# Twelve instead of ten token tiles of a second matrix product by 2x2 blocks, with the first block sum made by an accumulating DMA

## Chip, core and metric

The kernel runs on one core of one Trainium2 chip. The metric is the device time of one execution in microseconds (us), lower is better. Three runs of the kernel before took 453.23, 453.87 and 454.25 us; their median is 453.87 us. Work is done by TensorE (PE, with its weight loads as PEld), VectorE (DVE), ScalarE (ACT) and GpSimd (POOL); SyncE (SP) issues most DMAs.

## What is computed

One transformer-like block on x of 2048 tokens by 448 channels, all in float32. A linear-attention part comes first; then a token-mixing MLP, whose two products are what matters here:

```python
h = _layernorm(x, axis=-1) * (1 + cb) + sb
h = _layernorm(h, axis=-1)                        # inside _B_ref
u = jnp.einsum("bsd,sf->bdf", h, w1) + b1         # first product over tokens, F = 1792
u = _gelu(u)
y = jnp.einsum("bdf,fs->bds", u, w2) + b2         # second product: 1792 -> 2048 tokens
x = x + gb * y.transpose(0, 2, 1)
```

The second product, y^T = w2^T u, is the stage that is changed: 16 tiles of 128 tokens by 448 channels, each a sum over 14 blocks of 128 hidden rows.

## The kernel before

**Precision.** A float32 operand is cut into a high part, rounded to the fast matmul type float32r, and a low part, the rest. `split` (lines 75 to 77) does it: ACT rounds (L76), DVE subtracts (L77).

**Plain tiles.** `load1`, `split1` and `mult1` (lines 967 to 983) take one block of 128 hidden rows for `n` neighbouring token tiles: one DMA from w2 (tile `q`, L969), one split into `qw`, and for each token tile three matmuls of 448 columns (`acc3`, lines 740 to 742: high x high, high x low, low x high). A tile pair (`n` = 2) therefore has 14 such steps of six matmuls, a single tile 14 steps of three. `out1` adds the finished tile to x (L1005) and stores it.

**Tiles by 2x2 blocks.** Two token tiles, and the hidden blocks in pairs (seven pairs), are taken together by a scheme with seven block products in place of eight and with sums of blocks ahead of them. The group index is `q` (tiles 2q and 2q+1), the product index `m` from 0 to 6. `load_quads` (L883 to L890) loads four block columns a11, a12, a21, a22 of w2, each as two DMAs of 4 and 3 blocks (256 and 192 KB, L889). The left operands of the products are, in order, a11, a12, s2, s1, s3, s4, a22, with s1 = a21 + a22, s2 = s1 - a11, s3 = a11 - a21, s4 = a12 - s2. `split7` (L906) cuts operand m into `a11h`/`a11l` and so on and then makes the sum that the table `PRODS` (L901) names beside it, on DVE (`sub`, L896). `mult7` (L916) runs one product: seven pairs of a matmul of 448 columns (high part, L928) and one of 224 columns (low part, L929), 14 matmuls. `out7` (L945) takes results away: ACT copies the accumulator at m = 0, 2, 3 (L934), DVE adds at m = 1, 4, 5 (`out2`, L938 to L940) and at m = 6 (L962, L963); tile 2q is stored after m = 5 and tile 2q+1 after m = 6 (L943, on SP's queue).

**Order.** All instructions are issued in the order in which the Python code runs (a manual schedule), one queue for each engine. Of the 16 token tiles, 0 to 9 go by blocks (`NS7 = 5` groups) and 10 to 15 by plain steps, as pairs (10, 11), (12, 13) and singles 14 and 15. The list `order` (lines 1009 to 1017) starts with 8 plain steps, goes on with the 35 products, among which 38 plain steps are spread evenly, and ends with 10 plain steps of tile 15:

```python
for n, (kind, p) in enumerate(order):
...
        load2(n + LOAD2)
        split2(n + SPLIT2)
        if n < len(order) - LAST:
            (mult7 if kind == "s" else mult1)(*p)
            (out7 if kind == "s" else out1)(*p)
```

So at entry n the loads are issued 12 entries ahead (`LOAD2`), the splits, with their sums, 4 ahead (`SPLIT2`), then the matmuls of entry n, then its results. A store waits on SP's queue for DVE, and the loads behind it in the queue wait with it. `fetch_x` (L1043) brings a parked x tile back. Tiles live in 76 equal slots of SBUF; a load also waits until the last reader of its slot is done.

**Ahead of the stage.** The first product over tokens (L740 to L742 with `up`) runs until about 319 us of the profile; `finish_u` (lines 842 to 875) turns its results into the right operands of the second product, and its last jobs run on ACT and DVE until about 329 us. POOL issues accumulating DMAs earlier in the kernel (L244, L376, L399, L405), each adding one SBUF tile into another; in this stage it issues none.

Of the kernel before, what the change touches and what calls it, by code (L numbers as in the profile page):

```python
# [11 lines left out]
ALU = mybir.AluOpType  # L12
# [5 lines left out]
NF = F // P  # L18
# [26 lines left out]
def block_kernel(ctx: ExitStack, tc: tile.TileContext, x, wqkv, wo, w1, b1, w2, b2, c, wmod, out):  # L45
    nc = tc.nc
# [15 lines left out]
    def slot(name, w=D, dt=F32, parts=P):  # L62
        return slots.tile([parts, w], dt, name=name, tag="slot", padded_shape=[P, 512])

    def tslot(name, dt=F32, parts=P, w=D):
        return tok.tile([parts, w], dt, name=name, tag="tok", padded_shape=[P, 512])
# [469 lines left out]
    for t in range(3, NT):  # L536
# [38 lines left out]
        if t == 4:  # L575
            for g in range(4):
                w = tslot(f"wo{g}", parts=G)
# [184 lines left out]
    for i in range(NT + LAG):  # L762
# [13 lines left out]
        t = i - LAG  # L776
# [54 lines left out]
    uparts = ctx.enter_context(tc.tile_pool(name="uparts", bufs=1, reuse_waits="tile"))  # L831
    HD = D // 2
    PAIRS, RS = NF // 2, ((0, 4), (4, 3))
    NS7 = 5
    uw, uops, ufull = {}, {}, {}

    def u_parts(r, name, src):
# [42 lines left out]
    raw2, hilo, acc2, cop = {}, {}, {}, {}  # L880
    QUADS = {"a11": (0, 0), "a12": (1, 0), "a21": (0, 1), "a22": (1, 1)}

    def load_quads(q):  # L883
        for name, (fo, to) in QUADS.items():
            raw2[q, name] = []
            for r0, n in RS:
# [2 lines left out]
                nc.sync.dma_start(w.rearrange("p (r c) -> p r c", c=P), w2v[fo, :, r0:r0 + n, c0:c0 + P])  # L889
                raw2[q, name].append(w)  # L890

    def sub(q, out, a, b, op=ALU.subtract, into=None):
        res = []
        for i, (r0, n) in enumerate(RS):
            w = raw2[q, into][i] if into else slot(f"{out}_{q}_{r0}", n * P)
            nc.vector.tensor_tensor(w, raw2[q, a][i], raw2[q, b][i], op=op)  # L896
            res.append(w)
        raw2[q, out] = res


    PRODS = (("a11", "b11", 0, ("s1", "a21", "a22", ALU.add)), ("a12", "b21", 1, ("s2", "s1", "a11")),  # L901
             ("s2", "t2", 0, ("s3", "a11", "a21", ALU.subtract, "a21")),
             ("s1", "t1", 2, ("s4", "a12", "s2", ALU.subtract, "a12")), ("s3", "t3", 0, None),
             ("s4", "b22", 2, None), ("a22", "t4", 0, None))

    def split7(q, m):  # L906
        a, _, _, add = PRODS[m]
        hilo[q, m] = []
        for w, (r0, nr) in zip(raw2[q, a], RS):
            h, l = slot(f"{a}h_{q}_{r0}", nr * P, F32R), slot(f"{a}l_{q}_{r0}", nr * P, F32R)  # L910
            split(w, h, l)
            hilo[q, m].append((h, l))
        if add:
            sub(q, *add)

    def mult7(q, m):  # L916
        a, b, k, _ = PRODS[m]
        opens = m in (0, 1, 3)
        if opens:
            acc2[q, k] = bank(f"y{q}_{k}")  # L920
        ps = acc2[q, k]
        closes = m in (1, 5, 6)
        cut = hilo.pop((q, m))
        for r in range(PAIRS):
            (h, l), i = cut[r // 4], r % 4
            w, wh = uops[b, r]
            s = slice(i * P, (i + 1) * P)
            nc.tensor.matmul(ps[:, :D], h[:, s], w, start=opens and r == 0, stop=False, skip_group_check=True)  # L928
            nc.tensor.matmul(ps[:, :HD], l[:, s], wh, start=False, stop=closes and r == PAIRS - 1,  # L929
                             skip_group_check=True)  # L930
# [76 lines left out]


    sevens = [(q, m) for q in range(NS7) for m in range(7)]
    plains = [(t, n, f) for t, n in ((10, 2), (12, 2), (14, 1), (15, 1)) for f in range(NF)]  # L1010
    LEAD, TAIL = 8, 10
    order = [("p", p) for p in plains[:LEAD]]
    mid = plains[LEAD:len(plains) - TAIL]
# [32 lines left out]
    for o0, n in W1G[1:]:  # L1046
# [5 lines left out]
        for r in range(first, NT):  # L1052
# [4 lines left out]
            if xleft and k % 2:  # L1057
                t = xleft.pop(0)
# [13 lines left out]
    for n, (kind, p) in enumerate(order):  # L1072
        if jobs:
            jobs.pop(0)()
        while xleft:
            t = xleft.pop(0)
# [42 lines left out]
```

## Time and profile before

| What | Value |
|---|---|
| Runs | 453.23, 453.87, 454.25 us; median 453.87 |
| The profiled execution | 452.57 us, of which the span of the core is 450.8 us; 1.77 us lie around it |
| PE busy in the span | 446.0 us (99%), granted clock 1.0 |
| Second product, first plain step to last product by blocks | 319.46 to 440.04 us |
| The 10 last plain steps, with the split-up last tile | 440.04 to 447.95 us |

Times in the profile count from the start of the span. A line of a group or timeline names the engine, the line of the code, the operation, and the output and input tiles by their names (`a11h` is the high part of a11, `y` an accumulator of a block product, `yp` one of a plain step). A matmul's duration in the timeline is its time in the pipeline; what it costs a stream of matmuls is the distance from its start to the next one's start.

### The profile page before, as it was taken

The page shows a single profiled execution, that of the slowest core. Times are in us where ns is not written, and L with a number is a line of the kernel's source. Part 1 is how long each engine was busy: PE and PEld are TensorE (multiplying, and loading weights), DVE is VectorE, ACT ScalarE, POOL GpSimd, SP SyncE. Part 2 cuts the span into 40 slices and gives each one's busy share as a digit, 9 for nine tenths or more (in the row PEclk, how much of TensorE's full clock was granted, in tenths as well). Part 3 has the DMA queues.
Part 4 walks back from the last instruction along what each step waited for, and adds up shares of the span by engine and source line. Part 5 has one row for each costly group of instructions (what it writes and reads, how often), then busy time and mean ns, then how long its engine had stood idle before and what let it go on. Part 6 is the DMA issues. An engine that isn't in the chain of part 4 may idle for free.

```text
span 450.8 us, 7295 instructions
## 1 busy us (share of the span) xinstructions
PE 446.0 (99%) x2385; PEld 411.0 (91%) x2385; DVE 356.0 (79%) x774; ACT 250.1 (55%) x559; POOL 89.0 (20%) x162
## 2 busy tenths in 40 slices
PE   9999999999999999999999999999999999999997
PEld 8689999989899999999999999999999999999997
DVE  5797787888899899896469677539696978798993
ACT  2659877755656576767675345236546262536350
POOL 2124675620014345554300000000000000000000
PEclk9999999999999999999999999999999999999999
DMA  8949899985200003222407463417960674628313
GB/s 216 308 113 205 148 188 248 223 203 163 72 0 2 23 25 104 62 49 48 138 28 242 135 203 100 132 36 233 279 184 24 197 224 125 168 100 254 111 58 100
DMA packets 60551, 61.64 MB, mean 137 GB/s; under 512 B 9376, under 2 KB 53856, under 8 KB 60512
## 3 DMA queue, kind: packets, MB, share of 16 engines
q1 hardware_dynamic: 54896, 52.45, 39.1%
q0 software_dynamic: 5616, 8.72, 11.8%
q8 instruction: 19, 0.31, 0.3%
q14 instruction: 20, 0.16, 0.1%
HBM read 45.09 MB, written 7.34 MB: 116 GB/s over the span
## 4 chain that ended last, share of the span: by engine, by line
PE 92%; POOL 3%; issue 3%; DVE 1%; ACT 0%; POOLq 0%; DVEq 0%
PE y L928 11%; PE up L742 10%; PE up L741 10%; PE up L740 10%; PE op L689 9%; PE qp L333 7%; PE y L929 6%; PE kp L333 4%; PE cacc L420 4%; PE yp L740 4%; PE yp L742 4%; PE yp L741 4%; PE warm L141 2%; PE tq L673 2%; POOL rs L289 1%
## 5 line engine op out<-in xcount | busy, mean ns | idle before, releaser
L742 PE MATMUL up<-h2h,pl 128*128 128x448 f32 x224 | 81.4, 363 | 0.0
L741 PE MATMUL up<-h2l,ph 128*128 128x448 f32 x224 | 81.2, 363 | 0.0
L740 PE MATMUL up<-h2h,ph 128*128 128x448 f32 x224 | 80.8, 361 | 0.0
L77 DVE TENSOR_TENSOR pl<-pr,ph 128x512 fp32r<-128x512 f32 (+1 forms) x60 | 36.2, 614 | 11.1 <-ACT ph L76 7.8
L741 PEld LDWEIGHTS up<-h2l,ph 128*128 128x128 f32 x224 | 42.1, 188 | 3.1
L740 PEld LDWEIGHTS up<-h2h,ph 128*128 128x128 f32 x224 | 41.9, 187 | 3.0
L742 PEld LDWEIGHTS up<-h2h,pl 128*128 128x128 f32 x224 | 42.0, 188 | 2.4
L76 ACT ACTIVATE ph<-pr 128x512 fp32r<-128x512 f32 (+1 forms) x60 | 32.7, 569 | 12.9 <-PE up L741 11.1
L934 ACT ACTIVATE cc<-y 128x448 f32<-128x448 f32 x15 | 8.2, 545 | 56.1 <-PE y L929 47.9
L740 PE MATMUL yp<-uw,qw 128*128 128x448 f32 x81 | 29.8, 367 | 0.0
L742 PE MATMUL yp<-uw,qw 128*128 128x448 f32 x81 | 29.4, 363 | 0.0
L741 PE MATMUL yp<-uw,qw 128*128 128x448 f32 x81 | 29.4, 363 | 0.0
L689 PE MATMUL op<-wph,pth 112*128 112x448 f32 x64 | 24.5, 383 | 0.0
L420 PE MATMUL cacc<-pkh,xh 128*128 128x448 f32 x64 | 24.3, 379 | 0.0
L76 ACT ACTIVATE qw<-q 128x256 fp32r<-128x256 f32 (+1 forms) x56 | 18.9, 353 | 8.0 <-DMA q<-in_B_w_dram 7.5
L689 PE MATMUL op<-wpl,pth 112*128 112x448 f32 x64 | 23.2, 363 | 0.0
L689 PE MATMUL op<-wph,ptl 112*128 112x448 f32 x64 | 23.2, 362 | 0.0
L420 PE MATMUL cacc<-pkl,xh 128*128 128x448 f32 x64 | 23.2, 362 | 0.0
L333 PE MATMUL kp<-wh,hl 128*128 128x448 f32 x60 | 21.6, 365 | 0.6 <-DVE hl L77 0.6
L77 DVE TENSOR_TENSOR qw<-q,qw 128x256 fp32r<-128x256 f32 (+1 forms) x56 | 18.8, 350 | 3.8 <-ACT qw L76 3.8
L333 PE MATMUL kp<-wh,hh 128*128 128x448 f32 x60 | 21.6, 366 | 0.0
L333 PE MATMUL qp<-wh,hh 128*128 128x448 f32 x60 | 21.6, 366 | 0.0
(214 smaller groups left out, 1233.2 us busy)
## 6 DMA issues: line engine op xcount, KB each, us to landing
pr<-in_B_w_dram SPq DMA_DIRECT2D x48, 256.0 KB, 3.0
a<-in_B_w_dram SPq DMA_DIRECT2D x20, 256.0 KB, 4.9
wm<-in_w_mod_dram SPq DMA_DIRECT2D x24, 196.0 KB, 4.9
a<-in_B_w_dram SPq DMA_DIRECT2D x20, 192.0 KB, 5.1
x<-in_A_x_dram SPq DMA_DIRECT2D x16, 224.0 KB, 4.5
xpark<-x SPq DMA_DIRECT2D x16, 224.0 KB, 1.9
q<-in_B_w_dram SPq DMA_DIRECT2D x28, 128.0 KB, 3.5
xb<-xpark SPq DMA_DIRECT2D x16, 224.0 KB, 3.9
```

The lines of the kernel that those rows point to most:

```text
L76: nc.scalar.activation(hi, full, AF.Copy)
L77: nc.vector.tensor_sub(lo, full, hi.bitcast(F32))
L141: nc.tensor.matmul(warm[:, :P], ones, ones, start=True, stop=True)
L333: nc.tensor.matmul(o, a[:, ch * P:(ch + 1) * P], b, start=(n == 0), stop=(n == 10))
L420: nc.tensor.matmul(cacc[ch][:, :D], a[:, s], b, start=(t == 0 and i == 0), stop=(t == NT - 1 and i == len(todo) - 1))
L673: nc.tensor.transpose(tps[t][:G, g * P:(g + 1) * P], pn[:, g * G:(g + 1) * G], ident)
L689: nc.tensor.matmul(opb[t][:, :D], a[:, s], b, start=(n == 0), stop=(n == 11))
L740: nc.tensor.matmul(ps[:, :D], hi[:, sl], mh, start=first, stop=False)
L741: nc.tensor.matmul(ps[:, :D], hi[:, sl], ml, start=False, stop=False)
L742: nc.tensor.matmul(ps[:, :D], lo[:, sl], mh, start=False, stop=last)
L928: nc.tensor.matmul(ps[:, :D], h[:, s], w, start=opens and r == 0, stop=False, skip_group_check=True)
L929: nc.tensor.matmul(ps[:, :HD], l[:, s], wh, start=False, stop=closes and r == PAIRS - 1, skip_group_check=True)
```

## The change

```diff
-    NS7 = 5
+    NS7 = 6
...
                 nc.sync.dma_start(w.rearrange("p (r c) -> p r c", c=P), w2v[fo, :, r0:r0 + n, c0:c0 + P])
                 raw2[q, name].append(w)
 
+        raw2[q, "s1"] = raw2.pop((q, "a21"))
+        for w, a in zip(raw2[q, "s1"], raw2[q, "a22"]):
+            nc.gpsimd.dma_start(w, a, accum_op=ALU.add)
+
...
-    PRODS = (("a11", "b11", 0, ("s1", "a21", "a22", ALU.add)), ("a12", "b21", 1, ("s2", "s1", "a11")),
-             ("s2", "t2", 0, ("s3", "a11", "a21", ALU.subtract, "a21")),
+    PRODS = (("a11", "b11", 0, None), ("a12", "b21", 1, ("s2", "s1", "a11")),
+             ("s2", "t2", 0, ("s3", "a22", "s2", ALU.subtract, "a11")),
              ("s1", "t1", 2, ("s4", "a12", "s2", ALU.subtract, "a12")), ("s3", "t3", 0, None),
              ("s4", "b22", 2, None), ("a22", "t4", 0, None))
...
-    plains = [(t, n, f) for t, n in ((10, 2), (12, 2), (14, 1), (15, 1)) for f in range(NF)]
+    plains = [(t, n, f) for t, n in ((12, 2), (14, 1), (15, 1)) for f in range(NF)]
```

Tiles 10 and 11 go from plain steps to a sixth group of block products. The list `order` has 42 products by blocks with 24 plain steps among them, where it had 35 with 38; its 8 first and 10 last entries stay plain steps of the same shapes. The sum s1 = a21 + a22 is no longer made by DVE: right behind the eight loads of a group, POOL issues two accumulating DMAs (256 and 192 KB) that add a22 into a21's tiles, which are s1 from then on. As a21 is gone, s3 is made as a22 - s2, which is the same a11 - a21, into a11's tiles. The number of sums on DVE is three for each group, where it was four. The matmuls of one product, the loads of one group and the results' way out are as they were.

## The prediction

> **What bounds the kernel now.** I read the busy shares and the chain that ended last first (both on the profile's page).
>
> ```profile
> span 450.8 us, 7295 instructions
> ...
> PE 446.0 (99%) x2385; PEld 411.0 (91%) x2385; DVE 356.0 (79%) x774; ACT 250.1 (55%) x559; POOL 89.0 (20%) x162
> ...
> PE 92%; POOL 3%; issue 3%; DVE 1%; ACT 0%; POOLq 0%; DVEq 0%
> ```
>
> PE is busy throughout and the chain runs over it: time goes away only where PE has less to do, and comes back only where something makes PE wait. Next the busy time in two stretches: the whole mix of block products and plain steps, and in it the fourth group of block products (q = 3) with its single plain steps.
>
> ```profile
> 329.06:440.04 110.98, 110.98 (x659) 104.84 (x658) 94.52 (x204) 50.49 (x124) 0.00 (x0) 1.00 0.48 142
> 400.70:420.98 20.28, 20.28 (x124) 19.17 (x122) 18.69 (x43) 10.00 (x25) 0.00 (x0) 1.00 0.61 176
> ```
>
> Columns: length, then busy PE, PEld, DVE, ACT, POOL, then clock, DMA share, GB/s. PE has no gap at all, at clock 1.00. The second engine is DVE: 94.52 us of 110.98, in the late group 18.69 of 20.28. So I ask two things: how much PE work goes, and whether DVE and what feeds it still keep ahead.
>
> **PE's work.** A busy sum misleads for pipelined matmuls; I take distances between starts in PE's timeline.
>
> ```profile
> 437.86 0.36 PE L928 MATMUL y<-ut,a22h 128*128 128x448 f32 x1
> 438.06 0.27 PE L929 MATMUL y<-ut,a22l 128*128 128x224 f32 x1
> 438.17 0.37 PE L928 MATMUL y<-ut,a22h 128*128 128x448 f32 x1
> 438.38 0.26 PE L929 MATMUL y<-ut,a22l 128*128 128x224 f32 x1
> ...
> 440.46 0.36 PE L742 MATMUL yp<-uw,qw 128*128 128x448 f32 x1
> 440.66 0.36 PE L740 MATMUL yp<-uw,qw 128*128 128x448 f32 x1
> ```
>
> A 448-column matmul costs 0.20 us, a 448 and 224 pair 0.31 (437.86 to 438.17). Plain: 0.60 for a single step, 1.20 for a pair step. From 319.46 (first plain step) to 440.04 (end of the last product) are 120.58 us: 8 x 1.20 ahead, then 20 pair and 18 single steps (24.0 + 10.8), which leaves 76.18 for 35 products, 2.177 each.
> - Removed: 14 pair steps, 84 matmuls, 16.80 us. Added: seven products, 98 matmuls, 7 x 2.177 = 15.24 us. **Net -1.56 us.** Single products read 2.18 to 2.21 us in the timeline, which gives -1.3; fewer changes between the two kinds of matmul (24 plain steps in between, not 38) may give some 0.2 more. I keep -1.3 to -1.75.
> - By the Trainium skill (TensorE: Matmul & The Clock Gate, section Back-to-back issue gap) an isolated warm matmul of N columns costs N/2.4 + 2.5 ns: 189 and 96 ns, and the net would be -1.9 us. It adds that at small N the formula under-counts, for want of the weight load; the 0.11 us here for 224 columns agree with that, and the trace's price stands.
>
> So the gain is small because the block scheme adds more, shorter matmuls than it takes away.
>
> **DVE's work.** The split and sum of one operand are two instructions back to back:
>
> ```profile
> 419.15 1.15 DVE L77 TENSOR_TENSOR a11l<-a,a11h 128x512 fp32r<-128x512 f32 x2
> 420.23 1.15 DVE L896 TENSOR_TENSOR s<-a,a 128x512 f32<-128x512 f32 x2
> 421.30 0.28 DVE L77 TENSOR_TENSOR qw<-q,qw 128x128 fp32r<-128x128 f32 x1
> ```
>
> Each pair of instructions occupies 1.07 us (419.15 to 420.23 to 421.30). The line of `s<-a,a` goes: 5 x 1.07 = -5.4. Added: a sixth group with 7 splits and 3 sums (10.7), three `out2` of 1.39 (417.76 to 419.15) and 0.72 for L962, L963: +15.6; removed 14 pair-step splits at about 0.34 and two L1005 of 0.65: -6.1. Net +4.1 us, hidden behind PE if it fits: 98.6 of 109.4. What counts is the late group: PE needs 7 x 2.177 + 4 x 0.60 = 17.64 us (four plain steps to a group, eight before), DVE 18.69 - 1.07 - four splits of 0.25 = 16.6. That leaves 1.0 us for waits, where 1.6 were left before. Laid out in DVE's order (splits four entries ahead, then the results, which wait for PE), DVE is then never later than some 1.0 us ahead of a product's start (s3, m = 4) and 2.0 ahead for s2. Before, the splits of q = 3 and 4 ended only 0.3 to 1.4 us ahead, and PE did not stall. I cost it at nothing. ACT (10.00 of 20.28) only loses work, and the tail keeps its 10 steps; their last two loads now stand ahead of the last store instead of behind it.
>
> **The accumulating DMA.** It takes 1.07 us off DVE, but s2 = s1 - a11 now waits for eight loads and then two DMAs. Behind the s2 sum in DVE's queue stand L962 and L963, which finish tile 2q-1 (group q-1); for them waits that tile's store on SP's queue, and behind the store stand the loads of group q+1.
>
> ```profile
> SPq L943 <- DVE xb L963: 6.8, 4, 2.3
> ```
>
> So it is a loop, one turn per group. From the end of L963: store, one q load and two x loads take 1.9 us to the first group load (419.24 to 419.70 and 404.76 to 406.62). First issue to last landing of the eight loads took 9.3 to 10.7 us, median 9.5 (406.62 to 416.11). Then the sums, L; then the second half of the s2 sum 0.55, and L962, L963 0.72. Total 12.7 + L, and it must be under PE's 17.64: **L may be 5.0 us.** No accumulating DMA runs in this stage before; the nearest rows are POOL's earlier ones:
>
> ```profile
> pkl<-pk POOLq DMA_DIRECT2D x11, 224.0 KB, 4.2
> xl<-h POOLq DMA_DIRECT2D x11, 192.0 KB, 4.4
> pl<-pr POOLq DMA_DIRECT2D x4, 256.0 KB, 4.3
> ```
>
> Single ones took 3.0 to 6.6 us, the long ones being the second of two issued together at a full DMA share (91.83, 6.2 us). The second sum here is issued as the last load lands, at a DMA share falling from 0.97 to that of a few 64 KB loads. I take L = 4.6: 0.4 us spare per turn, no stall. At 3.0 the result is the same; at 6.6 see the first rival. Groups 0 and 1 are loaded long ahead (311 and 325 us, s2 needed near 329 and 348), group 2 has about 2.5 us to spare; the loop binds for groups 3 to 5. POOL issues nothing else; the loads for tiles 10 and 11 (28 of 128 KB less 8 group loads) are no longer.
>
> By the Trainium skill (DMA: Bandwidth & Descriptors, Anatomy of one DMA) a DMA of POOL takes about 2.0 us plus bytes over 436 GB/s, 2.6 us for 256 KB; the rows above say 4.3, and the measurement decides. By it the loop would have 2 us more to spare, with the same sum.
>
> **Sum.** -1.56 + 0 + 0 = -1.56 us. Against the profiled execution: span 450.8 to 449.2, execution 452.57 to 451.0. That execution lay 1.3 us under the median; runs will be compared by medians, so 453.87 - 1.56 = **452.3 us**.
>
> **Rivals.** The measurement can tell about 0.2% (0.9 us) from no change; faster means under 453.0, slower over 454.8.
>
> 1. *The late sum* (slower). The loop above, with L near the long rows. Place: the s2 sum of groups 3 to 5. For: the loop is nearly as long as PE's turn, and splits have 1 us to spare. Against: DMA is quieter here than where 6 us were seen. At L = 6.6 each of three turns lags 1.6, 4.9 in all, less the 1.0 DVE is ahead: +3.8 - 1.56, **456.1 us**. Gain and loss cancel when 3 x (L - 5.0) - 1.0 = 1.56, at L = 5.85; 454.8 us is reached near L = 6.1. The Trainium skill (SBUF — State Buffer, section Who interferes with whom and the box above it) has a rule that would make L long: POOL can't write descriptors while DVE runs an operation in a two-port mode, though tensor_tensor has none. DVE's operations here are all TENSOR_TENSOR, and POOL's DMAs between 60 and 95 us landed in 3.1 to 6.6 us beside a DVE busy 83% (29.16 of 35 us), so I add little for it. Chance 0.20.
> 2. *DVE becomes the bound.* If it can't do with 1.0 us of waiting per group and idles 1.6 as before, its turn is 18.2: 0.55 more than PE's, over four groups 2.2, less the 1.0 it is ahead: +1.2, **453.5 us**, no difference that can be told. For: denser block products (two in a row without a plain step). Against: the layout above. Chance 0.20, with smaller lags of the sum.
> 3. *The change doesn't do what it says:* products side by side cost PE more than among plain steps. At 2.30 us each, 42 of them would cost 5.2 us. Nothing in the timeline shows a neighbour's effect over 0.02 us. Chance 0.02, counted as slower, with 0.18 of the first rival.
>
> The forecast has 0.58. Its own range is 451.5 (-1.75, and 0.6 for the runs' scatter, 453.23 under 453.87) to 452.9. The first rival reaches from 453 to 456; I stop at 455.2, which leaves out about 1 in 8 above. Faster 0.58, same 0.22 (rival 2 and mild forms of rival 1), slower 0.20.
>
> **What will show it.** PE busy without gaps from 319 to about 438.5 us, products at 2.18 us: the first step is right. Total of DVE's busy time up by about 4 us and no PE wait on a split: the second. POOL's L894 landing within 5 us, and the s2 sum never waiting long for it: the third. PE gaps ahead of s2, s3 (m = 2, 4) in groups 3 to 5 with the s2 sum waiting for a DMA would be rival 1; the same gaps without such a wait, rival 2. I am wrong if a load or an x tile that I took for early waits in SP's queue.

## The result, and the profile after

The changed kernel takes **453.98 us** in the median of 22 runs (453.02 to 455.19); the kernel before, beside it, 453.01 us (22 runs, 452.13 to 454.25). Ratio 1.002, 95% interval 1.0012 to 1.0029: slower by about 1 us, where 1.6 us less had been forecast. The profiled executions took 453.25 us (span 451.5) and 452.57 us (span 450.8).

The page of the changed kernel (its line numbers are those of before plus 4 behind the change: L932 and L933 are the block matmuls, L966 and L967 the last adds of a group, L947 the store, L889 the group loads, L894 the accumulating DMA, L900 the sums):

```profile
span 451.5 us, 7367 instructions
...
PE 445.2 (99%) x2399; PEld 408.9 (91%) x2399; DVE 360.5 (80%) x779; ACT 254.6 (56%) x562; POOL 98.9 (22%) x174
...
PE 86%; DMA 6%; DVE 4%; issue 1%; SPq 1%; POOL 1%; ACT 0%; POOLq 0%; DVEq 0%; ACTq 0%
```

PE is busy for 0.8 us less while the span is 0.7 us longer, so PE now waits. The chain, which was PE 92% with no DMA in it, holds 6% DMA and 4% DVE. The busy time in stretches shows where (length, then PE, PEld, DVE, ACT, POOL, clock, DMA share, GB/s); the second line is one turn of PE, from 0.73 us behind the start of the first product of q = 4 to the same place in q = 5; the third goes on from there to the first of the 10 last plain steps:

```profile
329.19:440.91 111.72, 111.07 (x676) 104.07 (x674) 99.19 (x210) 55.63 (x129) 8.77 (x10) 1.00 0.61 164
405.16:423.07 17.91, 17.91 (x112) 16.93 (x111) 16.00 (x35) 9.30 (x21) 1.75 (x2) 1.00 0.73 198
423.07:441.63 18.56, 17.91 (x107) 16.02 (x106) 15.63 (x35) 8.83 (x24) 0.00 (x0) 1.00 0.37 107
```

Only the last stretch has a gap: 0.65 us by these busy sums, which hide a part of it: a matmul lasts 0.36 us in the pipeline, the next starts 0.2 us after it, and so the first 0.16 us of a delay leave no idle time (at 428.03 below, 0.24 us of idle time for a start that is 0.4 late). What the weight loads wait for, from 329 us on (us in total, times, longest); in the kernel before, this view has no line at all:

```profile
PEld yp L742 <- DVE qw L77: 0.8, 1, 0.8
PEld y L933 <- DVE s2l L77: 0.6, 1, 0.6
PEld y L933 <- DVE s3l L77: 0.3, 1, 0.3
```

PE's timeline at these places. A gap is a distance between starts over the usual 0.21 and 0.11 us: the first pair of s2 takes 428.24 - 427.43 = 0.81 us for 0.31, and the third matmul of a plain step starts 0.77 us after the second:

```profile
427.43 0.36 PE L932 MATMUL y<-ut,s2h 128*128 128x448 f32 x1
428.03 0.37 PE L933 MATMUL y<-ut,s2l 128*128 128x224 f32 x1 [0.24 <-DVE s2l L77]
428.24 0.37 PE L932 MATMUL y<-ut,s2h 128*128 128x448 f32 x1
...
432.53 0.36 PE L741 MATMUL yp<-uw,qw 128*128 128x448 f32 x1
433.30 0.47 PE L742 MATMUL yp<-uw,qw 128*128 128x448 f32 x1 [0.41 <-DVE qw L77]
```

With s3's first pair late too, these gaps come to 1.38 us, all in the last group (128.45 - 127.07 in the table below). DVE, which PE waits for, waited itself just before, for the two halves of the accumulating DMA:

```profile
421.58 1.15 DVE L77 TENSOR_TENSOR a12l<-a,a12h 128x512 fp32r<-128x512 f32 x2
423.87 0.69 DVE L900 TENSOR_TENSOR s<-a,a 128x512 f32<-128x512 f32 x1 [1.14 <-DMA a<-a]
425.36 0.56 DVE L900 TENSOR_TENSOR s<-a,a 128x384 f32<-128x384 f32 x1 [0.79 <-DMA a<-a]
425.83 0.38 DVE L966 TENSOR_TENSOR xb<-y,xb 128x224 f32<-128x224 f32 x1
426.25 0.39 DVE L967 TENSOR_TENSOR xb<-y,xb 128x224 f32<-128x224 f32 x1
...
427.29 1.15 DVE L77 TENSOR_TENSOR s2l<-s,s2h 128x512 fp32r<-128x512 f32 x2
```

In brackets: 1.14 and 0.79 us idle, 1.9 us in a row on an engine that had 1 us to spare. Behind the sum stand L966 and L967, and behind them, in SP's queue, a store and the next group's loads:

```profile
407.81 0.34 SPq L947 DMA_DIRECT2D out_dram<-xb  x1
408.25 0.38 SPq L973 DMA_DIRECT2D q<-in_B_w_dram  x1
408.73 0.88 SPq L1047 DMA_DIRECT2D xb<-xpark  x2
409.70 2.55 SPq L889 DMA_DIRECT2D a<-in_B_w_dram  x5
...
426.67 0.34 SPq L947 DMA_DIRECT2D out_dram<-xb  x1
```

From store to store is one turn of the loop: 426.67 - 407.81 = 18.86 us (and 407.81 - 389.04 = 18.77 for the turn before). PE's turn is 17.91 us. The loop loses 0.9 us in each of these two turns (and 0.3 in the one before), so the lead of the s2 split, counted from the end of its first half to the start of its product, shrinks: 2.11, 1.79, 0.94 us in groups 2, 3 and 4. In group 5 it is 0.54 us late. That last step is 1.48 us and not 0.9: in the last group DVE has one more instruction ahead of the s2 split, the add that finishes plain tile 14 (L1009, at 426.76), and it takes 0.53 us. In the kernels without a stall the same add takes the lead from 2.10 to 1.57 us.

**Where the time went.** From the marks of both traces (first plain step of the stage, last matmul's start, last landing, end of the span) the stage and its end can be laid out for every kernel but e10, whose traced execution is told of below:

| kernel | median us | ratio to before (95%) | stage start | start to last matmul | last landing to end |
|---|---|---|---|---|---|
| before | 453.01 | 1 | 319.46 | 128.21 | 0.96 |
| after | 453.98 | 1.0020 (1.0012 to 1.0029) | 319.59 | 128.45 | 1.32 |
| e1 six groups, sum on DVE | 452.38 | 0.9994 (0.9983 to 1.0005) | 319.68 | 127.40 | 1.33 |
| e2 five groups, sum by DMA | 452.75 | 0.9998 (0.9988 to 1.0007) | 319.69 | 128.21 | 0.95 |
| e3 six groups, no sum | 452.40 | 0.9984 (0.9972 to 0.9996) | 319.36 | 127.42 | 1.33 |
| e4 sum's loads first | 452.25 | 0.9985 (0.9975 to 0.9995) | 319.49 | 127.42 | 1.33 |
| e5 loads two entries earlier | 456.09 | 1.0073 (1.0059 to 1.0087) | 320.93 | 130.12 | 1.32 |
| e6 stores from POOL | 452.55 | 0.9998 (0.9986 to 1.0009) | 319.83 | 127.07 | 1.71 |
| e7 = e4, one SP DMA fewer | 451.77 | 0.9980 (0.9969 to 0.9992) | 319.49 | 127.07 | 0.91 |
| e8 = e7, last loads earlier | 451.78 | 0.9974 (0.9962 to 0.9986) | 320.00 | 127.07 | 0.91 |
| e9 = e1, both mends | 452.34 | 0.9993 (0.9982 to 1.0003) | 320.26 | 127.39 | 0.91 |
| e11 = after, one SP DMA fewer | 454.94 | 1.0033 (1.0018 to 1.0049) | 321.18 | 129.27 | 0.90 |
| e12 = e8 again | 451.86 | 0.9983 (0.9971 to 0.9996) | 319.51 | 127.07 | 0.91 |

Each ratio is against runs of before on the same chip; those medians lay between 452.82 and 453.01. From last matmul to last landing are 2.1 us everywhere. The fifth column has a floor, 127.07 us, that four runs reach: it is the stage with no wait of PE, and 1.14 us under before. So after against before, by span: 0.13 earlier work, -1.14 PE's work, +1.38 gaps, +0.36 at the end: **+0.73 us**, as the spans say (451.5 - 450.8).

### The profile page after: what moved, and what is told of

Its sections match the earlier page's. It is cut to its first block, busy times and chain, and to the rows that moved or that the text cites. A ratio compares the mean times of both kernels' runs of the same rounds, so it can differ in the third digit from the quotient of the medians.

```text
span 451.5 us, 7367 instructions
## 1 busy us (share of the span) xinstructions
PE 445.2 (99%) x2399; PEld 408.9 (91%) x2399; DVE 360.5 (80%) x779; ACT 254.6 (56%) x562; POOL 98.9 (22%) x174
## 4 chain that ended last, share of the span: by engine, by line
PE 86%; DMA 6%; DVE 4%; issue 1%; SPq 1%; POOL 1%; ACT 0%; POOLq 0%; DVEq 0%; ACTq 0%
PE up L742 10%; PE up L741 10%; PE up L740 10%; PE y L932 9%; PE op L689 9%; PE qp L333 7%; PE kp L333 7%; PE cacc L420 7%; PE y L933 4%; DMA a<-a 2%; DMA a<-in_B_w_dram 2%; PE yp L742 2%; PE yp L740 2%; PE yp L741 2%; PE tq L673 2%
## 5 line engine op out<-in xcount | busy, mean ns | idle before, releaser
L894 POOL DMA_DIRECT2D a<-a x12 | 10.6, 958 | 185.8 <-DVE qw L77 96.6
L76 ACT ACTIVATE s2h<-s 128x512 fp32r<-128x512 f32 (+1 forms) x12 | 6.8, 578 | 26.7 <-DVE s L900 26.6
L76 ACT ACTIVATE qw<-q 128x128 fp32r<-128x128 f32 (+1 forms) x42 | 13.0, 336 | 15.4 <-DMA q<-in_B_w_dram 15.4
L333 PE MATMUL qp<-wh,hl 128*128 128x448 f32 x60 | 21.4, 363 | 0.0
L848 DVE TENSOR_TENSOR u<-u,mod 128x448 f32<-128x448 f32 x14 | 8.7, 621 | 16.0 <-ACT u L847 16.0
L677 ACT ACTIVATE pth<-tq 112x512 fp32r<-112x512 f32 x16 | 9.6, 599 | 20.5 <-PE tq L673 17.7
```

The source lines that it names most:

```text
L76: nc.scalar.activation(hi, full, AF.Copy)
L333: nc.tensor.matmul(o, a[:, ch * P:(ch + 1) * P], b, start=(n == 0), stop=(n == 10))
L677: nc.scalar.activation(phs[t][0], tps[t][:G, :], AF.Copy)
L894: nc.gpsimd.dma_start(w, a, accum_op=ALU.add)
```

## The experiments

Theory: *the late sum*. PE's saving is real (-1.1) and is eaten by the loop of store, loads, accumulating DMA, s2 sum. Rivals: DVE is simply too full with six groups; the accumulating DMA slows other work wherever it stands; the loads wait for buffers, not for the store.

**e1, the sum on DVE.** Six groups, the rest of the change undone:

```diff
-        raw2[q, "s1"] = raw2.pop((q, "a21"))
-        for w, a in zip(raw2[q, "s1"], raw2[q, "a22"]):
-            nc.gpsimd.dma_start(w, a, accum_op=ALU.add)
-    PRODS = (("a11", "b11", 0, None), ...
+    PRODS = (("a11", "b11", 0, ("s1", "a21", "a22", ALU.add)), ...
```

> Sixth group alone: s1 is again made by DVE, no accumulating DMA. Changes are given against the kernel before; the changed kernel is at about +0.95 us. The theory of the late sum (loads wait for a store, the store for DVE, DVE for the sum of the loads before) has no loop here, but DVE gets 1.07 us more per group, 17.7 us of work beside 17.9 us of PE: +0.3 to +1.5 us. The rival (DVE is simply too full, whatever feeds it) expects clearly worse than the changed kernel, +2 us or more, because DVE has 6.4 us more to do. If it lies under -0.8 us, both are wrong and the accumulating DMA itself is the whole loss.

Measured: no difference from before (0.9994, -0.3 us), by the two ratios 1.2 us faster than after. Both forecasts are missed: the rival's clearly, and also mine of +0.3 to +1.5, which took DVE for nearer its limit than it is. The splits of s2 are still 0.50 us ahead in the last group, s3 is 0.24 late, and PE waits for little:

```profile
PEld y L929 <- DVE s3l L77: 0.3, 1, 0.3
PEld yp L742 <- DVE qw L77: 0.2, 1, 0.2
```

(This kernel's lines are numbered as in before.) So "DVE too full" falls: with 6.4 us more of sums than in the changed kernel (6 x 1.07) it costs PE 0.33 us (127.40 against the floor).

**e3, no sum at all.** It leaves out the computation of s1 (a21 alone stands in for it), so DVE and POOL have neither the sum nor the wait:

```diff
-        for w, a in zip(raw2[q, "s1"], raw2[q, "a22"]):
-            nc.gpsimd.dma_start(w, a, accum_op=ALU.add)
```

> Sixth group, and the sum s1 is left out altogether (a21 is taken for s1, so the outputs differ): neither POOL nor DVE makes it; DVE's work is that of the changed kernel. Late sum: s2 waits only for loads, which land some 5 us sooner than the sums did; PE runs without stalls and the whole matmul gain shows, -1.3 us against before (14 pair steps, 16.8, for seven products of 2.21 us, 15.5). Rival, DVE too full: the same DVE work, so the same stalls, about +0.9 us.

Measured: 0.9984, 0.7 us under before. The gaps ahead of the products are gone, s2 is 1.57 us ahead in the last group. Half of the expected 1.3 is missing, and the table says where: 0.35 in the tail (127.42 against the floor), 0.37 at the end.

**e4, the sum's loads first.** All work kept; only the order of the eight loads of a group changes, so that the sums start four loads earlier:

```diff
-    QUADS = {"a11": (0, 0), "a12": (1, 0), "a21": (0, 1), "a22": (1, 1)}
+    QUADS = {"a21": (0, 1), "a22": (1, 1), "a11": (0, 0), "a12": (1, 0)}
```

> The changed kernel with a21 and a22 loaded first and a11, a12 last; nothing else. Late sum: the two sums start some 4.5 us earlier against the group's first load, the loop of store, loads, sums and s2 falls from about 18.2 to under 14 us, PE doesn't stall: -1.3 us against before. Rival, DVE too full: unchanged, about +0.9 us. A third way: a11 now lands last but two and its split waits, then ACT's a11h shows waits for a DMA and it is at +0.5 us or more.

Measured: 0.9985, the same as with no sum at all. DVE goes from the a12 split through the s2 sum without a wait (compare 421.58 to 425.83 above):

```profile
421.47 1.15 DVE L77 TENSOR_TENSOR a12l<-a,a12h 128x512 fp32r<-128x512 f32 x2
422.54 1.15 DVE L900 TENSOR_TENSOR s<-a,a 128x512 f32<-128x512 f32 x2
423.61 0.38 DVE L966 TENSOR_TENSOR xb<-y,xb 128x224 f32<-128x224 f32 x1
```

The DMA itself is no faster here: from the issue of the first sum to the landing of the second 6.1, 6.8, 5.9 and 5.3 us in groups 2 to 5, where the changed kernel has 4.5, 5.2, 5.3 and 6.0. It is only early. The same work with no gap left in the products is what shows the cause. In the tail the last load now counts: PE waits for the operand of f = 13, whose load was issued at 440.06, behind a store and an x load, and took 5.05 us. What the weight loads wait for in e4, all of it:

```profile
PEld yl L999 <- ACT qw L76: 0.3, 1, 0.3
```

**e5, all loads two entries earlier.**

```diff
-LOAD2, SPLIT2 = 12, 4
+LOAD2, SPLIT2 = 14, 4
```

> The changed kernel with loads issued 14 entries ahead in place of 12: in SP's queue the group loads then stand ahead of the store that waits for L967 (m = 6), behind the store of m = 5. Late sum: the loop is cut and loads go some 4 us earlier, -1.3 us against before, or somewhat less if loads now wait for slots. Rival, DVE too full: about +0.9 us as the changed kernel.

A miss: 1.0073, 3.3 us slower than before. The sums are early, but the x tiles of a group now stand behind its successor's eight loads in SP's queue, and DVE's adds wait for them:

```profile
DVE xb L943 <- DMA xb<-xpark: 8.5, 4, 2.6
```

and PE's weight loads for DVE, 3.05 us over the floor by starts:

```profile
PEld yp L742 <- DVE qw L77: 2.8, 3, 1.2
PEld y L933 <- DVE s3l L77: 0.9, 3, 0.3
```

The stage also began 1.3 us later than in the changed kernel, already so at 109 us of the span, in work that the edit does not touch; why is open.

**e2, the sum by DMA with five groups.** NS7 = 5 and tiles 10 and 11 by plain pair steps again, the accumulating DMA kept:

```diff
-    NS7 = 6
+    NS7 = 5
-    plains = [(t, n, f) for t, n in ((12, 2), (14, 1), (15, 1)) for f in range(NF)]
+    plains = [(t, n, f) for t, n in ((10, 2), (12, 2), (14, 1), (15, 1)) for f in range(NF)]
```

> Ten tiles by blocks as before, only the first sum made by the accumulating DMA. Loop theory: a group's turn on PE is here 7 products and 8 single plain steps, 7 x 2.21 + 8 x 0.60 = 20.3 us, and the loop of store, loads, sums, s2 took 12.7 + 6.1 = 18.8 at its slowest, so nothing stalls: the time of before, ratio 1.000 within 0.001, though DVE has 5.4 us less to do. Rival (the accumulating DMA costs by itself, wherever it stands: s2 late or engines slowed beside it): at least 0.5 us slower than before, with PE gaps ahead of s2.

Measured: 0.9998, and the stage takes 128.21 us as before to the hundredth. So the DMA does not slow other work, and its 5.4 us less on DVE are worth nothing there. Neither part of the change alone costs time (e1 and e2); the loss needs both, since only with six groups is PE's turn (17.91 us) shorter than the loop (18.8).

**e6, stores from POOL's queue.**

```diff
-        nc.sync.dma_start(of[t * P:(t + 1) * P, :], X[t])
+        nc.gpsimd.dma_start(of[t * P:(t + 1) * P, :], X[t])
```

> As after, but the finished tiles are stored from POOL's queue, so that no load stands behind a store. Loop theory: the loads of a group leave earlier, s2 and s3 are in time, the 1.4 us of PE gaps in the last group are gone and so is the 0.35 us in the tail, since the last two loads no longer follow a store: about 0.6 to 1.1 us faster than before, ratio near 0.998. Rival (the loads wait for buffers that PE and DVE free, the store only happens to stand there): the gaps stay, 0.2 to 0.4% over before less little. Second rival: a store from POOL holds its tile longer (4 us against 2 from SP), so that loads wait for the buffer of the stored tile: slower than after.

The loads of the last group, which left at 409.70 in the changed kernel, leave 12 us earlier, and in one go:

```profile
396.41 0.94 SPq L1047 DMA_DIRECT2D xb<-xpark  x2
397.52 4.91 SPq L889 DMA_DIRECT2D a<-in_B_w_dram  x8
```

No PE gap is left (127.07). So it was the store in SP's queue that held them, not their buffers. Some loads do now wait for the slot of a tile that POOL stores (18.6 us in SP's queue, four waits), but not long enough to hold PE up. The time is nevertheless that of before (0.9998), so the forecast of 0.998 is missed: the end became 1.71 us long, 0.4 more than in the changed kernel. Against the changed kernel stage and end give -1.38 + 0.39 = -1.0 us, of which the traces' spans show 0.7 (450.8 against 451.5), as the stage began 0.24 us later.

**e7, one SP DMA fewer.** After the last landing SP goes through its eight DMA semaphores one after the other: in e4's semaphore records at 449.07 (the one of the last store, which landed at 449.05), then 449.13, 449.19 and so on to 449.50, about 0.06 us each. SP's DMAs take the eight in turn, so the number of SP's DMAs in the whole program decides which one the last store has. Before, there are 271, and it is the seventh; with the sixth group there are 265, and it is the first, so seven steps come after it rather than one. e7 is e4 with one early load moved, far from the end, which leaves 264, and the last store has the eighth:

```diff
-                nc.sync.dma_start(w, wo[g * G:(g + 1) * G, :])
+                (nc.sync if g else nc.gpsimd).dma_start(w, wo[g * G:(g + 1) * G, :])
```

> Sum quads loaded first, as in the earlier run of that edit (span 450.4 us), and one early load of wo moved from SP's to POOL's queue: one DMA fewer on SP, so that the last store's semaphore is the last of SP's eight and is looked at last at the kernel's end. Theory (the end costs 0.06 us for every check that follows that of the last store): from the last landing to the end of the span about 0.9 us instead of 1.3, 0.37 us off: span 450.0, ratio to before near 0.9977. Rival (the end does not depend on the turn of the semaphores): the span stays at 450.4.

Measured: landing to end 0.91 us instead of 1.33. SP's waits at the end of e7 show two short waits, for the last two stores each in its turn:

```profile
SPq L1119 <- DMA out_dram<-xb: 0.7, 2, 0.4
```

where the changed kernel has one long one, with the other steps behind it:

```profile
SPq L1119 <- DMA out_dram<-xb: 1.1, 1, 1.1
```

The span fell by 0.8, not 0.4: the slow last load took 4.55 us instead of 5.05 this time, just enough for the tail to be without a wait.

**e8 and e12, the last loads earlier as well.**

```diff
-        load2(n + LOAD2)
+        load2(n + LOAD2 + (4 if n >= 66 else 0))
```

> The same, and the last loads of tile 15 leave four entries earlier, from the entry of the last group's third product on. Tail theory: the split of f = 13 is in time, the last matmuls of the tail don't wait, another 0.35 us off: span 449.6 us, ratio to before near 0.997 (1.3 us faster). Rival (the load itself is slow, 5 us, for a reason that does not lie in its place): the load takes 5 us wherever it stands, but earlier, so the stall goes all the same; only if PE has to wait elsewhere, because the loads take buffers earlier, does the gain not come.

> The mended kernel (sum quads first, one load of wo on POOL's queue, tile 15's last loads four entries earlier) once more, on one chip with the kernel above. Theory: no PE gaps, end 0.91 us after the last landing, stage start to end 130.1 us; ratio to before 0.997 to 0.998 as in its first run. Rival (the first run's ratio was luck of a chip, as the 0.9993 of the twin with the sum on DVE suggests, whose span from the stage's start is only 0.32 us longer): ratio 0.9985 or more.

Measured: 0.9974 and 0.9983, the stage at its floor both times. The loads of f = 12 and 13 leave at 431.4 and 431.8 us in e8 instead of 440; ACT has rounded their operands by 436.4, and DVE makes the low parts by 442.7, where in e4 the last one came at 445.8. In median e8 can't be told from e7 (451.78, 451.77): the mend only takes away the chance of a late load. The rival that this was luck of a chip is not excluded by the second ratio, but the traces are alike (127.07 and 0.91 both times). It beats both kernels: by medians 2 us under the changed one and 1 us under before.

**e9, the same mends with the sum on DVE**, e1 with the two edits just shown for e7 and e8 (the order of a group's loads as in before):

> Twelve tiles by blocks with the first sum on DVE, as in the earlier run of that edit (stage start to last matmul 127.39 us, where the mended kernel with the accumulating DMA took 127.07), with both mends: one load of wo moved to POOL's queue and tile 15's last loads four entries earlier. Theory (the accumulating DMA buys next to nothing once it is in time, since DVE's 5 us are hidden behind PE): end 0.42 us shorter than in the earlier run of the edit, 0.3 us behind the mended kernel with the DMA: ratio to before near 0.998. Rival (DVE without the DMA is so full that earlier loads and splits push results back): PE gaps over 0.5 us in the last group and a ratio of 0.9995 or more.

Measured: ratio 0.9993, worse than expected, though stage and end are as expected (127.39, and 0.91 at the end, 0.32 us behind e8). Against the mean of e8 and e12 (0.9978) it is 0.7 us slower, of which the stage explains 0.32; this execution's stage also began late, at 320.26. The intervals (0.9982 to 1.0003 here, 0.9971 to 0.9996 for e12) overlap. That the accumulating DMA brings 0.3 us is what the traces show; the times can't confirm it.

**e10 and e11, the end alone on the changed kernel.** After with e7's edit and nothing else:

> The changed kernel itself with nothing but the one load of wo moved to POOL's queue. End theory: from the last landing to the end of the span 0.91 us instead of 1.32, everything else as it was, the PE gaps of 1.4 us ahead of s2 and s3 in the last group too: 0.4 us under the changed kernel, ratio to before near 1.001. Rival (the shorter end of the earlier run came with its other edit, the order of the loads): 1.32 us again and a ratio near 1.002.

> The changed kernel with nothing but one load of wo moved to POOL's queue, once more, since the profiled execution of the earlier run had PE at half its pace throughout and so says nothing of the end. End theory: 0.91 us from the last landing to the end of the span instead of 1.32, PE gaps of about 1.4 us in the last group as in the changed kernel: 0.4 us under the changed kernel, ratio to before near 1.001. Rival: 1.32 us again, ratio near 1.002 (the earlier run gave 1.0023, interval 1.0007 to 1.0039).

e10's profiled execution had each matmul at 754 ns where the others have 361, so its rows say nothing; its ratio, which leaves that execution out, is 1.0023 (1.0007 to 1.0039). e11's end is 0.90 us, as the theory says, so the end does not hang on e4's order. But e11 as a whole is 1.0033, and the forecast of 1.001 is missed both times: the loop cost 2.20 us over the floor here, not 1.38. Its waits on the weight loads:

```profile
PEld yp L742 <- DVE qw L77: 1.6, 2, 0.8
PEld y L933 <- DVE s3l L77: 0.9, 3, 0.3
PEld y L933 <- DVE s2l L77: 0.4, 1, 0.4
```

In e11 the eight loads of group 3 took 10.7 us to the last landing (9.7 in after), and PE waits in groups 3, 4 and 5 alike. A loop that is longer than PE's turn hands each delay of a DMA on to PE. The times of e11 run from 452.1 to 456.0 us, but those of e12, without a gap, from 450.8 to 453.7, so that the scatter comes of the loop is not shown. (Its stage also began 1.6 us late, as in e5.) So the 0.4 us of the end could be seen in the trace and not in the time.

## Why the prediction was wrong, step by step

- **PE's net of -1.56: right in kind, mis-sized.** The floor says 127.07 - 128.21 = -1.14. I read 440.04 as the end of 38 plain steps of the mix, but two single ones still follow, to 441.26 (so the stretch from 440.04 to 447.95 holds 12 plain steps, not 10). So 35 products took 121.80 - 44.40 = 77.40 us, 2.211 each and not 2.177; in e7, where PE does not wait, 42 take 120.66 - 27.60 = 93.06, 2.216 each. 14 pair steps removed are 16.80, the products 93.06 - 77.40 = 15.66. Rival 3 (products side by side cost more) is out: 0.005 us each.
- **DVE's work: right.** Busy 356.0 to 360.5, +4.5 for the +4.1 forecast, and it was hidden. Rival 2 is refuted by e3, with the same work on DVE and no gap in the products, and by e1, where DVE has 6.4 us more and PE loses 0.3.
- **The accumulating DMA: the step that failed** is "I take L = 4.6: 0.4 us spare per turn, no stall". L was 5.3, 5.4 and 6.1 us in groups 3 to 5. The loop was right in its links (1.9 us to the first load; 9.7, 10.1 and 9.5 us for the eight loads, where 9.5 was taken; PE's turn 17.91 instead of 17.64), and the durations of single DMAs were right too:

```profile
a<-a POOLq DMA_DIRECT2D x6, 256.0 KB, 3.4
...
a<-a POOLq DMA_DIRECT2D x6, 192.0 KB, 4.9
```

  I had set L equal to one DMA. But POOL issues the second 0.8 us after the last load has landed, and the second of a pair is the long one: 0.8 + 4.5, + 4.6, + 5.3. This is how the pair stands in the timeline of the last group (the last load landed at 419.23, the sums at 423.85 and 425.33):

```profile
419.31 1.75 POOL L894 DMA_DIRECT2D a<-a  x2 [16.37 <-DMA a<-in_B_w_dram]
```

  The prediction knew that the second is long ("the long ones being the second of two issued together") and took the short rows because DMA would be quieter. It was quieter (a DMA share of 0.90 from 409.70 to 419.23, while the eight loads ran, and 0.64 from there to 425.33), and L was long all the same. That 4.6 is possible was no error: L was 4.6 in group 2 and 4.6 to 4.75 in groups 2 to 4 of e2, as 0.8 or 0.9 and a second DMA of 3.8. Why the second took 4.5 to 5.3 in groups 3 to 5 of the changed kernel stays open. There SP issued a store and a 64 KB load while the sums ran (384.79 and 385.23 in group 3), which it did not do in group 3 of e2; no run tested whether that is the reason. With 0.4 us to spare on a loop of 17 us whose parts scatter by 1 us, "no stall" should not have been the likeliest. By the Trainium skill (DMA: Bandwidth & Descriptors, Anatomy of one DMA) 256 KB would take some 2.6 us, an estimate; the runs show 3.3 to 5.8 for the first of a pair in groups 2 to 5, so the measurement decides, against the page.
- **Rival 1 was the outcome, in a mild form.** Its formula with the measured mean L of 5.6 gives 3 x 0.6 - 1.0 = +0.8 of stall; measured +1.38 (s2 of the last group late by 0.54, and a plain step and s3 behind it). That the two are near each other is in part luck: the turns lost 0.3, 0.9 and 0.9, and the add of tile 14 another 0.5, which the formula does not have.
- **The tail: half right.** The last loads do stand ahead of the last store, but behind the store before it and an x load. It cost nothing in the changed kernel, which was late anyway, and 0.35 in e3 and e4.
- **The end: not in the sum.** +0.36 us, in every kernel with six groups and SP's DMAs as they were. So even without a stall the change would have brought -1.14 + 0.36 = -0.8 us, half of the forecast; e3 and e4 measured -0.7.
- The base of 453.87 was a median of three runs, 0.9 us over that of 22. That shifted the forecast's number, not its sign.

## What to carry to other kernels

Before you give an engine's work to a DMA, write down the loop that closes through the queue behind it (store, loads, sum, the adds that release the next store) and compare its length with PE's turn; with less than the scatter of one DMA to spare, count on a stall. When two DMAs follow each other the wait is the spacing of their issues plus the second one (0.8 + 4.5 to 5.3 us here), not one DMA. The cure was an order, not less work: load first what the longest chain needs, and keep loads from standing behind a store that waits for results.

## What the runs showed of the hardware that was not expected

- The end of the kernel depends on the number of SP's DMAs: 0.91, 0.96 or 1.33 us from the last landing to the end, by the turn of the last store's semaphore among SP's eight (0.06 us for each that comes after it). With stores from POOL it was 1.71.
- A load of 64 KB issued at about 440 us (e3, e4, e7) or 441.54 (after) took 4.55 to 5.05 us, and the store behind it 4.6 to 5.0, while a load of the same size 0.4 us ahead took 2.3 to 2.4. In before, at 442.00, it took 2.3, in e1, at 440.37, 2.5, and in e11, at 443.94, 2.5 (the store behind it 4.2). In e8 the loads leave earlier and the store at 441.08 took 2.1. What makes it slow in some kernels was not settled.
- The stage began up to 1.6 us later in some executions (e5, e11), with the difference already there at 109 us; its cause was not tested.
